# A delta-rule recurrence with a gated MLP: the first phase written out as one plan for all engines

## The chip, the cores and the metric

The kernel runs on one core of one Trainium2 chip. The metric is device time in microseconds for one execution. The engines are PE (TensorE, matmuls and its weight loads), DVE (VectorE), ACT (ScalarE), POOL (GpSimd) and SP (SyncE, which here issues transfers). Each works through its own list of instructions in order and waits on semaphores for the others. The order of each list is settled when the program is built.

## The reference

The first part is a recurrence over 768 tokens for 4 batches of 8 heads, with a 40 x 40 state per head:

```python
for t in range(S):
    y[:, :, t] = np.einsum('bhd,bhde->bhe', rt, state)
    Sa = np.einsum('bhde,bhe->bhd', state, at)
    state_decay = state * wt[:, :, None, :] - np.einsum('bhd,bhe->bhde', Sa, bt)
    state = state_decay + np.einsum('bhd,bhe->bhde', vt, kt)
```

The second part takes y, with the heads side by side, as x (4 x 768 x 320):

```python
h = np.maximum(x @ w_in, 0.0)
u, v = (h[..., :d_ff // 2], h[..., d_ff // 2:])
v_n = (v - mu) / np.sqrt(var + 1e-06)
v_s = np.einsum('ts,bsd->btd', w_spatial, v_n) + b_spatial[None, :, None]
return ((u * v_s) @ w_out)
```

## The kernel before

**Phase 1** (from L211) works on chunks of 64 tokens. Two batches go together: a step s handles 16 heads, as two groups g of four units n, where a unit has one head in the lower 64 partitions (par 0) and one in the upper (par 1). There are 24 steps: 12 chunks for each pair of batches. Inside a chunk the recurrence is a triangular system, so each step falls into parts.

- *Preparation* of chunk q (prep_steps, L309): a load into `ein`, two running products over the decays on VectorE (S, L318, and Et, L328), a small transfer of the chunk's total decay to DRAM (scr, L326), and the scaled operands `at` (L335) and `sl` (L338). lprime (L348) multiplies them into 32 x 32 triangular blocks, and lblock (L363, eviction at L368) masks these into Lc.
- *Inverse* (invert, L373): for four chunks at once, VectorE transposes the blocks, does thirty pairs of a multiply (L381) and an add (L385), and transposes the result twice (X11 at L389, XT0 at L392).
- *Bulk* products that don't need the state: b_lka (L420) with its mask on VectorE (L439), b_h (L444), b_tok (L458), and b_l21, b_zt, b_x21 with b_xcopy, which put together the 64 x 64 inverse `xf` from 32-wide parts. `xf` is stored 128 wide, with the two heads of a unit as diagonal blocks.
- *Chain* (chain, L517): four stages for each group, handing on from one to the next. bp multiplies the state (L540) and ScalarE copies it to Rt (L546); ff (L551) is copied to ffs (L556), and POOL masks the h part of Rt (L559); xx (L566) multiplies by the inverse and goes back into Rt, up to step 5 as a ScalarE copy (L573) with a POOL mask (L574), later as a ScalarE copy of the last 40 columns (L580) and a VectorE multiply by a mask (L581); mp (L590) updates the state Mc on VectorE (L595, L596), which ScalarE copies into Ms (L598), 128 wide with two diagonal blocks; y is finished at L601 and scaled at L609.

The *MoE* input layer (the reference's x @ w_in) runs beside phase 1, from stored y, in units: m_u (L714, 48 units) and m_v (L671, 24 units, followed by the normalization). Its weights come as 64-bit words and are decoded by VectorE (decode64, L69). In both units the last of eight products reads 64 partitions. **Phase 2** (L105) multiplies by w_spatial (pg, L172 to L174) and w_out (po, L192).

The order of the work is the tile framework's planner's: the code emits the chain's stages and lists of tasks by numbered slots (eight a step, from the constants at the top), and the planner orders each engine's list by its own cost model, with phase 2 included. The one exception is the start, where VectorE keeps the written order. All preparations from chunk 4 on use one load buffer, `ein[0]`; the other three serve only the first four chunks. All transfers are issued by SP's queue.

## Time and profile before

| | |
|---|---|
| median of 3 runs | 806.27 us (805.7 to 807.37) |
| span of the profiled execution | 803.9 us |
| instructions | 24058 |
| PE busy | 661.0 us (82%), 10016 matmuls |
| DVE busy | 489.7 us (61%), 992 |
| ACT busy | 413.1 us (51%), 960 |
| POOL busy | 289.4 us (36%), 449 |
| moved by DMA | 78.23 MB, mean 97 GB/s |

The profiled execution's own time beside its span is not in the page; the median of the runs lies 2.4 us above the span. A row of the groups has the line, the engine, the operation, out<-in, the shapes and the count, then the busy time in us and the mean of one in ns, then the idle time of the engine before these instructions and what ended it. Matmul records overlap (each runs through the array while the next starts), so their durations add up to more than they take. One fp32 matmul shows as two records. In a row in order of time the first two numbers are its start and its length in us.

### The profile page before, as it was taken

What the parts mean: (1) busy time and instruction counts of PE and PEld (TensorE: products, weight loads), DVE (VectorE), ACT (ScalarE), POOL (GpSimd) and SP (SyncE); (2) the same over time, 40 slices, a digit from 0 to 9 for tenths busy, and PEclk for the clock granted to TensorE, in tenths of its full rate; (3) what the DMA queues carried; (4) which work ended last, traced back from release to release, by engine and by line L of the source; (5) the groups of instructions that cost most, each with busy time, mean ns of one, the idle gap of its engine ahead of it and who ended that gap; (6) DMA issues with size and microseconds to landing.
All of it is one profiled execution on the core that took longest, in us unless ns stands there. A gap on an engine that the chain in (4) does not pass through costs nothing.

```text
span 803.9 us, 24058 instructions
## 1 busy us (share of the span) xinstructions
PE 661.0 (82%) x10016; PEld 571.2 (71%) x10016; DVE 489.7 (61%) x992; ACT 413.1 (51%) x960; POOL 289.4 (36%) x449
## 2 busy tenths in 40 slices
PE   1620575865989687988899899999999999999997
PEld 1520464654777575876777778787878898999997
DVE  7849358897389563898459874987232753232221
ACT  6210454333767184665675577778877243232112
POOL 5320455443435132332142331212143587353221
PEclk9965678555999799898899999999999999999999
DMA  7631355442354545352554444333342655153001
GB/s 169 100 44 39 38 95 120 100 79 54 101 96 59 108 84 107 94 97 58 102 86 111 89 125 125 93 102 115 103 124 73 192 184 177 64 173 106 31 25 50
DMA packets 113944, 78.23 MB, mean 97 GB/s; under 512 B 46844, under 2 KB 103420, under 8 KB 111996
## 3 DMA queue, kind: packets, MB, share of 16 engines
q1 hardware_dynamic: 113836, 76.70, 40.9%
q8 instruction: 79, 1.29, 0.8%
q14 instruction: 29, 0.24, 0.2%
HBM read 56.16 MB, written 20.51 MB: 95 GB/s over the span
## 4 chain that ended last, share of the span: by engine, by line
PE 47%; DVE 19%; DMA 16%; ACT 6%; issue 5%; POOL 5%; SPq 1%; DVEq 0%; POOLq 0%; ACTq 0%
DMA ein<-in_early 10%; PE po L192 5%; PE pv L714 5%; PE bp L540 5%; PE pv L671 4%; DVE A L385 4%; DVE itmp L381 3%; PE pg L173 3%; PE pg L174 3%; PE pg L172 3%; PE ch L551 3%; PE bk L450 2%; PE bp L601 2%; DVE S L318 2%; PE ch L566 2%
## 5 line engine op out<-in xcount | busy, mean ns | idle before, releaser
L338 POOL TENSOR_TENSOR sl<-ein,S 128x512 f32<-128x512 f32 x44 | 56.6, 1305 | 99.3 <-DVE S L318 57.3
L385 DVE TENSOR_TENSOR A<-A,itmp 128x30 f32<-128x30 f32 (+9 forms) x180 | 77.2, 429 | 4.2
L381 DVE TENSOR_TENSOR itmp<-A 128x30 f32<-128x30 f32 (+9 forms) x180 | 73.2, 407 | 4.6
L551 PE MATMUL ch<-Rt,At 128*64 128x104 f32 x768 | 57.2, 270 | 12.7 <-issue 12.4
L318 DVE TENSOR_TENSOR_SCAN S<-ein,ends 128x528 f32<-128x528 f32 x24 | 30.8, 1282 | 58.3 <-DMA ein<-in_early 54.6
L176 DVE TENSOR_TENSOR g<-pg,bb 128x384 f32<-128x384 f32 x32 | 17.7, 555 | 77.9 <-PE pg L174 71.1
L172 PE MATMUL pg<-wsh,vh 128*128 128x384 f32 x192 | 65.1, 339 | 0.0
L173 PE MATMUL pg<-wsl,vh 128*128 128x384 f32 x192 | 64.8, 338 | 0.0
L174 PE MATMUL pg<-wsh,vl 128*128 128x384 f32 x192 | 64.7, 337 | 0.0
L566 PE MATMUL ch<-ffs,xf 128*128 128x104 f32 x384 | 58.9, 303 | 6.3 <-ACT ffs L556 6.1
L540 PE MATMUL bp<-lin,Ms 128*104 128x104 f32 x384 | 53.9, 295 | 8.9 <-DMA lin<-in_late 4.2
L335 POOL TENSOR_TENSOR at<-ein,Et 128x256 f32<-128x256 f32 x40 | 27.9, 718 | 87.7 <-DVE Et L328 30.4
L566 PEld LDWEIGHTS ch<-ffs,xf 128*128 128x128 f32 x384 | 52.4, 211 | 9.9 <-ACT ffs L556 7.5
L551 PEld LDWEIGHTS ch<-Rt,At 128*64 128x64 f32 x768 | 43.5, 143 | 19.7 <-issue 14.9
L546 ACT ACTIVATE Rt<-bp 64x416 f32<-64x416 f32 x96 | 48.9, 510 | 15.2 <-PE bp L540 13.3
L358 PE MATMUL bk<-at,sl 64*32 64x32 f32 x1536 | 28.3, 208 | 34.2 <-POOL sl L338 9.9
L540 PEld LDWEIGHTS bp<-lin,Ms 128*104 128x104 f32 x384 | 47.1, 201 | 12.8 <-issue 7.9
L66 POOL TENSOR_TENSOR gl<-g,gh 128x384 fp32r<-128x384 f32 x32 | 33.3, 1042 | 59.6 <-ACT gh L62 59.6
L559 POOL TENSOR_SCALAR_AFFINE_SELECT Rt<-Rt 64x256 f32<-64x256 f32 x96 | 42.0, 438 | 32.1 <-PE ch L551 26.7
L418 ACT ACTIVATE xf<-XT 32x256 f32<-32x256 f32 x96 | 39.7, 414 | 23.8 <-DVE XT L392 22.5
L358 PEld LDWEIGHTS bk<-at,sl 64*32 64x32 f32 x1536 | 21.2, 119 | 40.6 <-issue 25.6
L601 PE MATMUL bp<-Rt,tk 128*40 128x64 f32 x768 | 43.0, 236 | 7.5 <-DVE Rt L581 5.0
(130 smaller groups left out, 1677.4 us busy)
## 6 DMA issues: line engine op xcount, KB each, us to landing
ein<-in_early SPq DMA_DIRECT2D x46, 322.5 KB
lin<-in_late SPq DMA_DIRECT2D x48, 160.0 KB
uts<-ur SPq DMA_DIRECT2D x48, 128.0 KB
vns<-vr SPq DMA_DIRECT2D x24, 256.0 KB
raw<-vns SPq DMA_DIRECT2D x24, 256.0 KB
ut<-uts SPq DMA_DIRECT2D x24, 256.0 KB
Rt<-in_vtok SPq DMA_DIRECT2D x48, 80.0 KB
xs<-y SPq DMA_DIRECT2D x48, 80.0 KB
```

The lines of the kernel that those rows point to most:

```text
L172: nc.tensor.matmul(pg, lhsT=vh[:, dc], rhs=w_h, start=(i == 0), stop=False)
L173: nc.tensor.matmul(pg, lhsT=vh[:, dc], rhs=w_l, start=False, stop=False)
L174: nc.tensor.matmul(pg, lhsT=vl[:, dc], rhs=w_h, start=False, stop=(i == NT - 1))
L338: st["sl"] = sl_eng[g].tensor_tensor(out=sl[:, gp], in0=oth[:, gp, 1:], in1=sv[:, gp, 2:C + 2].unsqueeze(2).broadcast_to([P, NP, 2, C]), o ...
L358: nc.tensor.matmul(pl[o:o + HB, n, :], lhsT=sl[PR[par], n, par, cs], rhs=at[PR[par], n, cs], start=True, stop=True,)
L381: nc.vector.tensor_tensor(out=tp, in0=A[:, k + 1:, k:k + 1].broadcast_to([P, m, k]), in1=A[:, k:k + 1, 0:k].broadcast_to([P, m, k]), op=AL ...
L385: nc.vector.tensor_tensor(out=A[:, k + 1:, 0:k], in0=A[:, k + 1:, 0:k], in1=tp, op=ALU.add)
L540: nc.tensor.matmul(bp[LV, q, :], lhsT=Ms[:, n, LV], rhs=li[:, n, C:], start=(q == 0), stop=False, skip_group_check=True,)
L546: nc.scalar.activation(Rt[par][rows, gp, :], bp[rows], AF.Copy)
L551: nc.tensor.matmul(ff[PR[1 - par], q, :], lhsT=At[par][:, n, :], rhs=Rt[par][:, n, :], start=True, stop=True,)
L566: nc.tensor.matmul(xx[:, q, :], lhsT=xf[:, n, :], rhs=ffs[:, q, :], start=True, stop=True,)
L601: nc.tensor.matmul(bp[RR[par], q, 0:C], lhsT=tk[:, n, par, :], rhs=Rt[par][:, n, 0:C], start=False, stop=True, skip_group_check=True,)
```

## The change

Phase 1 is rewritten as one list of (time, function) entries, `plan`, with times in steps: at(3.55, c_xx, 3, 0) is stage xx of step 3. The list is sorted, and up to step 24 it is emitted inside a region in which **every** engine keeps the written order (`manual_schedule()` without a list of engines). What comes later, the rest of the MoE and phase 2, is still the planner's.

- Each stage of the chain is cut into its products (c_bp, c_ff, c_xx, c_mp, c_y) and their evictions (c_..._out), and the two groups run side by side: both groups' bp, then both groups' ff, with bulk products and MoE units between.
- The state Mc is kept 64 wide and read directly: bp is two 40-row, 64-column products a unit instead of one of 128 rows and 104 columns, and Ms and its ScalarE copies are gone. The inverse xf is 64 wide too: xx is two 64 x 64 products a unit instead of one 128 x 128. xf's first copies move from ScalarE to POOL (on ScalarE for chunk 0), three instead of four.
- The mask after xx is POOL's in every step (TRI_ACT = 99), after a ScalarE copy of all columns. The mask on h moves from the chain to b_h_out, over both groups at once.
- Preparations use two load buffers in turn, `ein[0]` and `ein[1]`, loads have 48 rows instead of 40 (64 in the first four), and from chunk 4 on POOL does at and sl in one instruction each. The first loads go over SP's and ScalarE's queues, with scan inputs first; the fills of buffers and the zeroing of Ms, Rt, lin go away. scr is stored straight from S.
- Each inverse is spread evenly over the plan: the first whole, right after the first four preparations, the second from 2.5 to 3.45, the later ones over some three steps each. XT0 is now written before X11.
- Weight decoding is cut into single instructions (steps 3.3 to 10.2). The MoE starts at step 11 with four units a step. Before it started at step 5 with six units every two steps. The last product of a unit reads 128 partitions.

The core of the diff (the bodies of ff, mp and y are those of chain, cut apart; bulk functions are split the same way):

```diff
-CHB, MMB = 3, 1
-MOE_LAG = 32
-DEC0, DEC_STEP, DEC_OPEN = 5, 1, 2
-PREP_LAG, LP0, LP1, LPB = 10, 1, 3, 6
-PREP_SLOTS, PREP_AFTER = (0, 0, 6, 7), (False, False, True, True)
-PREP_OFF = (3, 4, 5)
-INV_SLOTS = (15, 17)
-LKA_ACT, TRI_ACT = 1, 6
-FIRST_SLOTS = ((0, 2, 2), (4, 5, 5, 6, 11, 12, 13), (10, 11, 11, 12, 14, 14, 15))
-BULK_OFF = (0, 0, 0, 1, 3, 1, 4, 4, 3, 1)
-MOE_OFF = (2, 1, 2, 3, 3, 3, 8, 3)
+LKA_ACT, TRI_ACT = 2, 99
...
-def decode64(nc, pool, h, l, src, n, bufs=1):
-    raw = pool.tile([P, n], I64, name="d_raw", bufs=bufs)
+def decode64_steps(nc, pool, h, l, src, n, bufs=1):
+    raw = pool.tile([P, n], I64, name="d_raw", bufs=2)
     nc.sync.dma_start(out=raw, in_=src)
+    yield
...
-    late_pool = late_bufs.enter_context(tc.tile_pool(name="late", bufs=1))
-    ein = [p.tile([P, EW], F32, name=f"ein{i}") for i, p in enumerate((pin, late_pool, extra, extra))]
+    ein = [p.tile([P, EW], F32, name=f"ein{i}") for i, p in enumerate((pin, pin, extra, extra))]
...
-    Ms = const.tile([P, NU, P], F32, name="Ms")
-    Mc = const.tile([P, NU, E], F32, name="Mc")
-    xfs = [const.tile([P, NU, P], F32, name=f"xf{i}") for i in range(2)]
+    Mc = const.tile([P, NU, C], F32, name="Mc")
+    xfs = [const.tile([P, NU, C], F32, name=f"xf{i}") for i in range(2)]
...
-    def prep_load(s, i=0, rows=E, cols=slice(0, EW)):
+    def prep_load(s, rows, cols=slice(0, EW), i=None, queues=(nc.sync, nc.sync)):
+        t = ein[s % 2 if i is None else i]
         for par in range(2):
             o = par * 64
-            nc.sync.dma_start(out=ein[i][o:o + rows, cols], in_=early[par, s, 0:rows, cols])
+            queues[par].dma_start(out=t[o:o + rows, cols], in_=early[par, s, 0:rows, cols])
...
+    def strict(t, k):
+        nc.gpsimd.affine_select(
+            out=t, in_=t, pattern=[[0, k], [1, C]], base=0, channel_multiplier=-1,
+            compare_op=ALU.is_gt, fill=0.0,
+        )
...
+    def b_h_out(s, par):
+        ev = PR[1 - par]
+        Rt = Rts[s % 2]
+        nc.scalar.activation(Rt[par][ev, :, 0:C], st["ph", s][ev], AF.Copy)
+        strict(Rt[par][ev, :, 0:C], NU)
...
+    def b_xcopy(s, eng):
+        XT0, X11 = st["X", s // GS]
+        us = slice((s % GS) * NU, (s % GS) * NU + NU)
+        xf = xfs[s % 2]
+        eng(out=xf[:, :, HB:], in_=XT0[:, us])
+        for o in (0, 64):
+            eng(out=xf[o:o + HB, :, 0:HB], in_=XT0[o:o + HB, us])
...
+    def c_bp(s, g):
+        gp, ns = grp(g)
         li = lin[s % 2]
+        bp = ps_b.tile([P, NP, NR], F32, name=f"bp{g}")
+        for q, n in enumerate(ns):
+            for par in range(2):
+                nc.tensor.matmul(
+                    bp[PR[par], q, :], lhsT=Mc[RR[par], n, :], rhs=li[RR[par], n, C:],
+                    start=(q == 0), stop=False, skip_group_check=True,
+                )
+        st["bp", g] = bp
+    def c_bp_out(s, g):
+        gp, ns = grp(g)
+        Rt = st["blk", s][1]
+        for par in range(2):
+            nc.scalar.activation(Rt[par][PR[par], gp, :], st["bp", g][PR[par]], AF.Copy)
...
+    def c_xx(s, g):
+        gp, ns = grp(g)
+        xf = st["blk", s][3]
+        ffs = st["ffs", g]
+        xx = ps_c.tile([P, NP, NR], F32, name="ch")
+        for q, n in enumerate(ns):
+            for ev in PR:
+                nc.tensor.matmul(
+                    xx[ev, q, :], lhsT=xf[ev, n, :], rhs=ffs[ev, q, :], start=True, stop=True,
+                )
+        st["xx", g] = xx
+    def c_xx_out(s, g):
+        gp, ns = grp(g)
+        Rt = st["blk", s][1]
+        xx = st["xx", g]
+        for par in range(2):
+            ur, ev = PR[par], PR[1 - par]
+            if s < TRI_ACT:
+                nc.scalar.activation(Rt[par][ur, gp], xx[ev], AF.Copy, scale=-1.0)
+                strict(Rt[par][ur, gp, 0:C], NP)
+                continue
+            nc.scalar.activation(Rt[par][ur, gp, C:], xx[ev, :, C:], AF.Copy, scale=-1.0)
+            nc.vector.tensor_tensor(
+                out=Rt[par][ur, gp, 0:C], in0=xx[ev, :, 0:C],
+                in1=maskn[ev].unsqueeze(1).broadcast_to([64, NP, C]), op=ALU.mult,
+            )
...
+    def c_mp_out(s, g):
+        gp, ns = grp(g)
+        if s % CPB == CPB - 1:
+            if s < NS - 1:
+                nc.vector.memset(Mc[:, gp, 0:E], 0.0)
+            return
+        mp = st["xx", g][:, :, C:]
+        mn = jit.tile([P, NP, E], F32, name="mn")
+        nc.vector.tensor_tensor(out=mn[LV], in0=mp[LV], in1=Mc[LV, gp, 0:E], op=ALU.add)
+        nc.vector.tensor_tensor(
+            out=Mc[LV, gp, 0:E], in0=mn[LV], in1=st["scn"][LV, gp, :], op=ALU.mult
+        )
...
-        mm += [(xh[:, k, g, :], wl[:, k, vc]) for k in range(2)]
-        mm += [(xh[0:64, 2, g, :], wl[0:64, 2, vc])]
+        mm += [(xh[:, k, g, :], wl[:, k, vc]) for k in range(3)]
...
+    M1, M2, M3, M4 = 0.22, 0.46, 0.65, 0.80
+    for s in range(NS):
+        at(s + 0.02, scn_load, s)
+        for g in range(NB):
+            at(s + 0.00 + 0.05 * g, c_bp, s, g)
+            at(s + 0.04 + 0.05 * g, c_bp_out, s, g)
+            at(s + 0.30 + 0.05 * g, c_ff, s, g)
+            at(s + 0.34 + 0.05 * g, c_ff_out, s, g)
+            at(s + 0.55 + 0.05 * g, c_xx, s, g)
+            at(s + 0.60 + 0.05 * g, c_xx_out, s, g)
+            at(s + 0.74 + 0.02 * g, c_mp, s, g)
+            at(s + 0.755 + 0.02 * g, c_mp_out, s, g)
+            at(s + 0.86 + 0.04 * g, c_y, s, g)
+            at(s + 0.90 + 0.04 * g, c_y_out, s, g)
+            at(s + 0.95 + 0.01 * g, y_store, s, g)
+    for q in range(1, NS):
+        b = q - 1
+        for par in range(2):
+            at(b + 0.11 + 0.02 * par, b_copy, q, par)
+            at(b + 0.17 + 0.02 * par, b_lka_out, q, par)
+            at(b + 0.72 + 0.02 * par, b_h_out, q, par)
+            at(b + 0.40 + 0.03 * par, b_tok, q, par)
+            at(b + 0.43 + 0.03 * par, b_tok_out, q, par)
+        at(b + 0.115, b_lka, q)
+        at(b + 0.52, b_l21, q)
+        at(b + 0.54, b_l21_out, q)
+        at(b + 0.66, b_zt, q)
+        at(b + 0.68, b_zt_out, q)
+        at(b + 0.68, b_h, q)
+        at(b + 0.50, b_xcopy, q, p.tensor_copy)
+        at(b + 0.78, b_x21, q)
+        at(b + 0.81, b_x21_out, q)
+    for q in range(2, NS):
+        at(q - 2 + 0.14, lin_load, q)
+        at(q - 2 + 0.97, vtok_load, q)
+    LPO = 0.93
+    PREP = {4: 0.03, 5: 0.45, 6: 1.03, 7: 1.45, 8: 2.03, 9: 2.45, 10: 3.03, 11: 3.45}
+    for q in range(GS, NS):
+        t = PREP.get(q, q - 8 + 0.01)
+        at(t + 0.20, scan1, q)
+        at(t + 0.28, scan2, q)
+        at(t + 0.285, scr_store, q)
+        at(t + 0.29, at_mul, q, p)
+        at(t + 0.30, sl_mul, q, p)
+        if q + 2 < NS:
+            at(t + 0.50, prep_load, q + 2, 48)
+        at(t + LPO, lprime, q)
+        at(t + LPO + 0.05, lblock, q)
+    for g in range(1, NS // GS):
+        t0 = 2.5 if g == 1 else max(4.5, GS * g - 4 + 0.0)
+        t1 = GS * g - 1 + 0.45
         gen = invert(g)
+        for k in range(INV_N):
+            at(t0 + (t1 - t0) * k / (INV_N - 1), step, gen)
+    T_DEC, T_MOE = 4.2, 11
     for i in range(6):
+        gen = decode(1 - i // 3, i % 3)
+        for k in range(9):
+            at(T_DEC + i + k * 0.12 - (0.9 if k == 0 else 0), step, gen)
+    at(T_DEC + 5.9, open_act)
+    slots = [T_MOE + k // 4 + (M1, M2, M3, M4)[k % 4] for k in range(3 * NS)]
+    for j in range(NS // 2):
+        bq, i = j // 6, j % 6
+        own = slots[6 * j:6 * j + 6]
+        at(max(own[0] - 1.6, 2 * j + 2.1, T_DEC + 5.92), m_load, bq, i)
+        at(max(own[0] - 0.7, 2 * j + 2.7), m_split, bq, i)
+        for t, d in zip((own[0], own[1], own[3], own[4]), range(DH // P)):
+            at(t, m_u, d, bq, i)
+        for t, g in zip((own[2], own[5]), range(NB)):
+            at(t, m_v, g, bq, i)
+            at(t + 0.14, m_n1, g)
+            at(t + 0.42, m_root, g)
+            at(t + 0.48, m_n2, g)
+            at(t + 0.76, m_n3, g, bq, i)
...
-    with tc.manual_schedule(engines={mybir.EngineType.DVE}):
+    with tc.manual_schedule():
+        W, O = slice(0, WF), slice(WF, EW)
+        qs = (nc.sync, nc.scalar)
+        for cols, q in ((W, 0), (W, 1), (O, 0), (W, 2), (O, 1), (W, 3), (O, 2), (O, 3)):
+            prep_load(q, 64, cols, q, qs)
+        lin_load(0)
...
+        for q in range(GS):
+            scan1(q, q)
+            scan2(q)
+            if q:
+                scr_store(q)
+            at_mul(q, p)
+            sl_mul(q, p, g0)
+            sl_mul(q, v, g1)
+            lprime(q)
+            if q:
+                lblock(q - 1)
+            if q == 0:
+                b_copy(0, 0)
...
+        lblock(GS - 1)
+        lin_load(1)
+        vtok_load(1)
+        prep_load(4, 48)
+        prep_load(5, 48)
         for _ in invert(0):
             pass
...
+        plan.sort()
+        n = 0
+        while plan[n][0] < NS:
+            t, _, fn, args = plan[n]
+            fn(*args)
+            n += 1
+    for t, _, fn, args in plan[n:]:
+        fn(*args)
```

627 lines of the change are left out of this document (244 added, 383 removed).

## The prediction

> **What bounds the kernel now.** I read the page from the top, then the chain of waits, then stretches of the span, and last the groups of instructions.
>
> ```profile
> span 803.9 us, 24058 instructions
> PE   1620575865989687988899899999999999999997
> PEclk9965678555999799898899999999999999999999
> ```
>
> Each digit is a twentieth of 40 us. From the 23rd slice on (about 440 us) TensorE is busy nine tenths or more at full clock; before that it has holes, and for the first 200 us the granted clock is often 0.5 to 0.7. So there are two problems: an early part that waits, and a late part that is bound by TensorE.
>
> ```profile
> PE 47%; DVE 19%; DMA 16%; ACT 6%; issue 5%; POOL 5%; SPq 1%; DVEq 0%; POOLq 0%; ACTq 0%
> ...
> 51.06 1.26 DVE L318 TENSOR_TENSOR_SCAN S<-ein,ends 128x528 f32<-128x528 f32 x1 [12.60 <-DMA ein<-in_early]
> 76.44 1.86 DVE L392 STREAM_TRANSPOSE XT<-A 128x1024 f32<-128x1024 f32 x1
> 95.37 1.26 DVE L318 TENSOR_TENSOR_SCAN S<-ein,ends 128x528 f32<-128x528 f32 x1 [12.06 <-DMA ein<-in_early]
> 102.36 0.42 DVE L609 TENSOR_TENSOR y<-bp,Et 104x256 f32<-104x256 f32 x1 [1.22 <-PE bp L601]
> 205.56 0.39 DVE L609 TENSOR_TENSOR y<-bp,Et 104x256 f32<-104x256 f32 x1
> 484.63 0.42 DVE L609 TENSOR_TENSOR y<-bp,Et 104x256 f32<-104x256 f32 x1
> 616.75 0.42 DVE L609 TENSOR_TENSOR y<-bp,Et 104x256 f32<-104x256 f32 x1
> ```
>
> Transfers are a sixth of the chain. The lines below the dots are VectorE in order of time. It stops twice for 12 us, in the middle of the first inverse and again in step 0, for a scan whose load is not there. One buffer feeds every later preparation, so a load starts only when the products of the chunk before have been read. L609 ends a step's second group: step 0 at 102.8 us, step 3 at 205.9, step 15 at 485.0, step 22 at 617.2. The last seven of these steps took 132.1/7 = 18.9 us each. The stretches say what filled them (core time, then busy us of PE, PEld, DVE, ACT, POOL, each with its count, clock, DMA share, GB/s):
>
> ```profile
> 126.00:206.00 80.00, 51.39 (x843) 42.26 (x834) 68.08 (x127) 28.67 (x64) 34.63 (x39) 0.64 0.40 85
> 485.00:617.00 132.00, 130.12 (x2263) 107.67 (x2263) 74.30 (x181) 103.90 (x244) 31.22 (x68) 1.00 0.37 106
> 643.00:804.00 161.00, 156.43 (x928) 149.48 (x926) 47.85 (x83) 44.92 (x96) 67.89 (x80) 1.00 0.32 101
> ```
>
> Steps 2 and 3 are VectorE's: 68 of 80 us. Steps 16 to 22 are TensorE's: 130 of 132. So is what follows the last step.
>
> **Start and step 0.** The first inverse now follows the four first preparations with no later scan inside it. Before it ended at 76.44 + 1.86 = 78.3 us. I take away the wait of 12.6 and the scan pair in it (1.28 + 1.67 + 0.2 for the reciprocal, 3.2): 62 us. The four chunks are loaded with 64 rows instead of mostly 40, but on two queues and without VectorE's and POOL's fills; the inverse's start at about 31 us leaves that room. From the inverse to the end of step 0 it was 24.5 us, 12.1 of it the second wait: 12 left, a little less since the XT transpose is now first. **Step 0 ends at 73**, 30 earlier. Two buffers, each refilled nearly two steps ahead, hide the later loads; they cost at most the old wait if the load is late in steps 0 to 3.
>
> **VectorE's steps.** The rows (busy us, mean ns of one):
>
> ```profile
> L385 DVE TENSOR_TENSOR A<-A,itmp 128x30 f32<-128x30 f32 (+9 forms) x180 | 77.2, 429 | 4.2
> L381 DVE TENSOR_TENSOR itmp<-A 128x30 f32<-128x30 f32 (+9 forms) x180 | 73.2, 407 | 4.6
> L328 DVE TENSOR_TENSOR_SCAN Et<-ein,ends 128x528 f32<-128x528 f32 x24 | 40.0, 1667 | 0.3
> L439 DVE TENSOR_TENSOR At<-bk,maskp 64x512 f32<-64x512 f32 x46 | 31.7, 689 | 24.3 <-PE bk L426 23.5
> L318 DVE TENSOR_TENSOR_SCAN S<-ein,ends 128x528 f32<-128x528 f32 x24 | 30.8, 1282 | 58.3 <-DMA ein<-in_early 54.6 <-POOL wl L102 3.4 <-ACT wc L324 0.3
> L581 DVE TENSOR_TENSOR Rt<-ch,maskn 64x256 f32<-64x256 f32 x72 | 30.4, 422 | 27.6 <-ACT Rt L580 25.9
> L609 DVE TENSOR_TENSOR y<-bp,Et 104x256 f32<-104x256 f32 x48 | 19.8, 414 | 6.0 <-PE bp L601 5.7 <-remote 0.2
> L679 DVE BATCH_NORM_STATS2 bs<-vr 128x6 f32<-128x512 f32 x24 | 16.4, 683 | 13.4 <-ACT vr L673 13.2
> L596 DVE TENSOR_TENSOR Mc<-mn,scn 104x160 f32<-104x160 f32 x44 | 15.7, 357 | 0.3
> L700 DVE TENSOR_SCALAR vr<-vr,mv,q 128x512 f32<-128x512 f32 x24 | 14.8, 622 | 11.5 <-POOL q L695 11.0
> L595 DVE TENSOR_TENSOR mn<-ch,Mc 104x160 f32<-104x160 f32 x44 | 13.9, 317 | 11.5 <-PE ch L590 9.4 <-remote 1.8
> L389 DVE STREAM_TRANSPOSE X<-A 128x1024 f32<-128x1024 f32 x6 | 12.0, 1993 | 0.2
> L368 DVE TENSOR_TENSOR Lc<-bk,maskl 128x256 f32<-128x256 f32 x24 | 9.9, 411 | 11.1 <-PE bk L358 7.3 <-PE bp L540 3.7
> ...
> 100.00:200.00 100.00, 25.85 (x42) 0.65 0.44 89
> ```
>
> The last line is VectorE on the weight decoding alone: 25.85/6 = 4.3 us a block. A step's fixed work is 1.28 + 1.67 + 0.2 (one preparation) + 2 x 0.689 + 0.41 + 2 x (0.317 + 0.357) + 2 x 0.414 = 7.1, 7.6 with half a microsecond between instructions. An inverse is 30 x (0.429 + 0.407) + 3 x 2.0 = 31, 33 with its gaps. L581 goes away: its mask is POOL's now.
>
> - Step 1: two preparations, 11; TensorE has 13.4 (below): **14**.
> - Steps 2 and 3: two preparations each and the whole second inverse, 2 x 11.2 + 33 = 55; **57** with waits.
> - Steps 4 to 7: 30.4 + 33 + four decoded blocks at 4.5 = 82; **86**.
> - Steps 8 to 11: 30.4 + 33 + two blocks = 72; **76**.
> - Steps 12 to 15: 30.4 + 33 + four units of the MoE a step (0.683 + 0.622 and two small ones, 1.7 for three units, so 2.3 a step) = 73; TensorE needs the same there: **78**.
>
> The microsecond a step that I add in steps 2 to 11 is for hand-overs: VectorE's evictions of lka and of mp stand in a fixed order and wait if TensorE is late. While they wait, the scans and the inverse behind them wait too, and POOL's products behind those.
>
> **TensorE's steps.** The group of L', then rows in order of time, inside steps 16 and 17 and after the last step:
>
> ```profile
> L358 PE MATMUL bk<-at,sl 64*32 64x32 f32 x1536 | 28.3, 208 | 34.2 <-POOL sl L338 9.9
> ...
> 508.99 0.93 PE L551 MATMUL ch<-Rt,At 128*64 128x104 f32 x16
> 511.76 1.14 PE L566 MATMUL ch<-ffs,xf 128*128 128x104 f32 x8
> 522.42 0.98 PE L540 MATMUL bp<-lin,Ms 128*104 128x104 f32 x8
> ...
> 711.68 0.52 PE L714 MATMUL pv<-xh,wh 128*128 128x256 f32 x3
> 712.04 0.40 PE L714 MATMUL pv<-xl,wh 128*128 128x256 f32 x2
> 712.27 0.71 PE L714 MATMUL pv<-xh,wl 128*128 128x256 f32 x3
> 712.91 0.45 PE L173 MATMUL pg<-wsl,vh 128*128 128x384 f32 x1
> 713.19 0.34 PE L174 MATMUL pg<-wsh,vl 128*128 128x384 f32 x1
> ```
>
> The state and inverse products become sixteen pieces 64 wide. The nearest form is L551, sixteen in 0.93: xx gains 0.21 a group (0.4 a step), bp 0.05 (0.1). Bounds: half of 0.93 if two quadrants run at once, 1.14 if they gain nothing. The MoE's last product reads 128 rows instead of 64. The first five of the unit at 711.68 started in 0.59 us, 0.118 each, so eight should take 0.94; the next line's work started 1.23 later and then stumbled by 0.11 more (0.28 between starts where 0.17 is usual). That is 0.4 a unit, 1.2 for the three units of a step. A fourth unit a step adds a third of (2 x 0.94 + 1.8) = 1.2. The hand order also runs each product whole, where the planner cut several into parts with another form between; I count 13 fewer changes of form a step. Between nothing and 0.2 each (half of the 0.4); I take 1.1 a step, nearer to the lower end, as most changes are not to 64 rows of 128 columns. Sum: 18.9 - 0.4 - 0.1 - 1.2 + 1.2 - 1.1 = 17.3. L' (absent from step 16 on) adds at most 28.3/24 = 1.2, its records overlapping; I take 0.9. Without the MoE: 17.3 - 4.8 + 0.9 = 13.4.
>
> ScalarE had 103.9/7 = 14.8 a step here. It loses the Ms and xf copies and gains wider Rt copies and one unit's eviction: it stays under 15 of 17.3, but is the next to be late. POOL's rows, one mask and the preparation's product (shortest, median, longest):
>
> ```profile
> L574 POOL TENSOR_SCALAR_AFFINE_SELECT Rt<-Rt 64x256 f32<-64x256 f32 x24 | 11.4, 476 | 6.4 <-ACT Rt L573 5.5
> ...
> L338 POOL TENSOR_TENSOR sl<-ein,S x44: 1170/1184/2133, 8.4 to 469.7; 128x512 f32<-128x512 f32 x44
> ```
>
> POOL had 31.2/7 = 4.5 a step in the late stretch. It gets four masks at 0.48 and three xf copies that the trace does not show: nearest the mask, 0.4 each, at most 1.2 like the product. About 8 of 17.3, hidden by TensorE unless it holds a mask that mp waits for; with that cover gone, the 3.1 a step would show, 25 us over steps 16 to 23. The two masks of h replace four half as wide. **Steps 16 to 23: 8 x 17.3 = 138.**
>
> **The end.** The MoE starts at step 11 with four units a step: 52 of 72 done when step 23 ends, 20 left, 160 matmuls, and phase 2's 864. Before, 928 took 161 us, with 15 broken units (6 us) and 3 for the last store: 0.164 each. 1024 x 0.164 + 3 = **171**, 10 more than before.
>
> **Sum.** 73 + 14 + 57 + 86 + 76 + 78 + 138 + 171 = 693 us of span. The median stands 806.27 - 803.9 = 2.4 above the profiled span: **695 us**.
>
> **Rivals.**
>
> *The clock.* In steps 2 to 11 TensorE has 13.4 of some 22 us to do, with one hole of several microseconds before bp, while VectorE finishes. At 126 to 206 us the same picture had a clock of 0.64. Then 13.4 becomes 20.9, and VectorE waits for lka and mp, some 3 us a step for ten steps: 725. For it: that row. Against: slices of 0.8 and 0.9 later, with TensorE at eight tenths. The Trainium skill (TensorE: Matmul & The Clock Gate, Part 1: The HAM clock gate) says that one idle window of about 3.4 us sends the array to half clock; the trace agrees in kind with the 0.64 here.
>
> *VectorE and POOL in each other's way.*
>
> ```profile
> L328 DVE TENSOR_TENSOR_SCAN Et<-ein,ends x24: 1215/1258/2315, 6.5 to 463.0; 128x528 f32<-128x528 f32 x24
> ```
>
> The same scan takes 1.2 or 2.3 us, the same product on POOL 1.2 or 2.1: they sometimes exclude each other. My means contain that at today's load. POOL will have 8.6 a step in steps 2 to 15 (the two sl products 2.4, the two of at 1.4, the masks 3.6, the copies 1.2). If all of it fell on VectorE, and a third of it is in the means, these steps take 5.7 more: 14 x 5.7 = 80, 775. Against: most scans are at the short end. The Trainium skill (SBUF — State Buffer, Who interferes with whom) has it as a rule, that a VectorE instruction with two SBUF inputs shuts out one of GpSimd that reads SBUF; by it the masks moved from VectorE, which read PSUM, cost VectorE part of what they save.
>
> *Only the start gains.* If the planner already packed what comes after step 3 as well as can be, steps 0 to 3 end at 144 instead of 206 and the end is 10 longer: 806 - 62 + 10 = 754. For it: nines from 440 us. Against: between 206 and 440 the slices aren't full.
>
> *Slower: the hand order exposes every eviction.* TensorE's order is fixed, so a stage that finds its eviction undone stops all behind it. One group is bp 0.93, two copies, ff 0.93, a copy, xx 0.93, two copies and a mask, mp and its two VectorE instructions: about 8 us; both one after the other 16, bulk products 6, units 5: 27 a step. With 24 in steps 1 to 11: 73 + 264 + 12 x 27 + 171 = 832. It is slower than now once steps 1 to 23 average over (804 - 73 - 171)/23 = 24.3; I forecast 19.5. Against: three to five microseconds of other products stand between a stage and its successor.
>
> **Chances.** Forecast 0.54 (its own range 665 to 720: the form changes alone give -18 to +13, 64-wide pieces at half price another -13); clock 0.14; only the start 0.13; VectorE against POOL 0.10; exposed evictions 0.08; 0.01 that it ends level. Range 655 to 775. About 0.2% (1.6 us) is what a measurement can tell from no change. Faster 0.91, same 0.01, slower 0.08.
>
> **What would show it.** Right: no DMA wait ahead of scans after the start; the first inverse done near 62; steps 4 to 11 with VectorE over nine tenths busy, 16 to 23 with TensorE; y of step 23 at 522. Wrong: clock under 0.7 in steps 4 to 11; inverse instructions longer than 0.43 on average; TensorE below nine tenths in steps 16 to 23 with waits on ScalarE's copies or POOL's masks, which would put the fault in the hand order.

## The result and the profile after

The changed kernel takes 782.83 us (median of 4 runs, 778.59 to 784.71); the kernel before, timed beside it, takes 806.82. The ratio is 0.969, 95% interval 0.965 to 0.973: faster, but by 24 us and not by the 111 forecast, and 8 us above the range. Its profiled execution has a span of 776.9 us. From the page of the changed kernel:

```profile
span 776.9 us, 25305 instructions
PE   0434676567676976779899789999999999589997
PEclk9985967658877696789689779999999999989999
DMA  9360787737567664564545544435426352353001
```

TensorE is full from the 25th slice on, but for the 35th and 36th; before, it was full from the 24th on. The early slices are better but not full. The granted clock is mostly lower than before from the 11th to the 24th slice. The same execution cut where the forecast cut it (core time, busy us of PE, PEld, DVE, ACT, POOL with counts, clock, DMA share, GB/s):

```profile
0.00:82.00 82.00, 30.29 (x785) 26.49 (x786) 51.87 (x99) 22.30 (x47) 28.80 (x45) 0.85 0.51 97
82.00:108.00 26.00, 17.18 (x476) 15.34 (x463) 9.59 (x17) 10.68 (x22) 11.28 (x15) 0.80 0.87 92
108.00:172.00 64.00, 38.40 (x978) 34.64 (x966) 54.81 (x98) 21.25 (x44) 26.29 (x28) 0.68 0.64 89
172.00:260.00 88.00, 63.19 (x1591) 56.56 (x1588) 78.57 (x140) 43.31 (x91) 42.12 (x50) 0.77 0.67 108
260.00:354.00 94.00, 72.90 (x1611) 64.88 (x1612) 74.39 (x128) 47.24 (x97) 45.63 (x54) 0.76 0.52 88
354.00:453.00 99.00, 84.08 (x1714) 74.09 (x1712) 73.96 (x145) 52.60 (x114) 46.86 (x76) 0.82 0.52 114
453.00:599.00 146.00, 142.55 (x2728) 124.67 (x2727) 80.82 (x185) 106.27 (x227) 71.80 (x147) 0.99 0.46 133
599.00:777.00 178.00, 162.49 (x964) 157.47 (x962) 55.59 (x99) 47.91 (x103) 72.43 (x94) 0.98 0.31 99
```

These are step 0, step 1, steps 2 and 3, 4 to 7, 8 to 11, 12 to 15, 16 to 23, and the end. In steps 1, 8 to 11 and 12 to 15 no engine is full, so no engine's own work fills them, and waits decide. TensorE's longest wait between 82 and 600 us, and all of its waits that end with "issue" (engine, line, waited for: us in total, times, longest):

```profile
PE bp L528 <- DVE y L630: 22.2, 8, 8.8
PE bk L325 <- issue: 10.5, 6, 2.6
PE ch L593 <- issue: 7.1, 7, 2.0
PE bk L388 <- issue: 6.5, 3, 3.4
PE bk L434 <- issue: 5.8, 1, 5.8
PE bp L617 <- issue: 4.5, 2, 2.3
PE bk L470 <- issue: 2.8, 2, 1.9
PE bk L418 <- issue: 2.7, 3, 1.7
PE bp L528 <- issue: 2.0, 1, 2.0
PE bk L451 <- issue: 0.8, 1, 0.8
```

"issue" is a wait that nothing in the profile explains. The rows with it add up to 42.7 us. I call them **stops**. The kernel before has 14.3 us of them in the same steps (102 to 643 us there):

```profile
PE bk L358 <- issue: 7.3, 3, 4.8
PE bp L540 <- issue: 2.6, 2, 1.4
PE bk L510 <- issue: 2.1, 3, 0.9
PE bk L450 <- issue: 2.0, 1, 2.0
PE ch L551 <- issue: 0.3, 1, 0.3
```

One stop of the changed kernel, in TensorE's order of time, step 11:

```profile
329.50 0.63 PE L388 MATMUL bk<-at,sl 64*64 64x64 f32 x16
333.58 0.69 PE L388 MATMUL bk<-at,sl 64*64 64x64 f32 x8 [3.44 <-issue]
```

It stops for 3.44 us within a group of 16 independent products (32 records). VectorE's eviction of this group waits 5.5 us (the longest of five between 192 and 354 us, below), and the step takes 26.4 us where its neighbours take 21.4 and 21.6.

```profile
DVE At L408 <- PE bk L388: 8.4, 5, 5.5
```

Start and step 15 have waits of their own. VectorE at chunk 3, then POOL behind it, then ScalarE in step 15:

```profile
29.91 1.26 DVE L282 TENSOR_TENSOR_SCAN S<-ein,ends 128x528 f32<-128x528 f32 x1 [8.84 <-DMA scr<-S]
41.27 0.42 DVE L336 TENSOR_TENSOR Lc<-bk,maskl 128x256 f32<-128x256 f32 x1 [7.65 <-PE bk L325]
41.73 1.94 DVE L344 STREAM_TRANSPOSE A<-Lc 128x1024 f32<-128x1024 f32 x1
```

```profile
36.42 1.37 POOL L395 TENSOR_SCALAR_AFFINE_SELECT Rt<-Rt 64x512 f32<-64x512 f32 x2 [10.04 <-ACT Rt L427]
```

```profile
444.79 0.84 ACT L52 ACTIVATE wsh<-raw 128x768 fp32r<-128x768 f32 x1 [7.24 <-DMA raw<-in_wspT]
```

S has two buffers, and scr is stored straight from it, so chunk 3's scan waits until the store of chunk 1 has read the buffer. Then POOL's products of chunk 3 stand behind the masks of h in the fixed order. The first inverse starts at 41.7 us, not 31.

Of two kernels below (the splits held behind step 16, and the first run with 40-row loads) the profiled execution was a disturbed one; their ratios are of undisturbed runs.

### The profile page after: what moved, and what is told of

Same layout as the page of the kernel before. It is cut to its first block, busy times and chain, and to the rows that moved or that the text cites. A ratio compares the mean times of both kernels' runs of the same rounds, so it can differ in the third digit from the quotient of the medians.

```text
span 776.9 us, 25305 instructions
## 1 busy us (share of the span) xinstructions
PE 611.1 (79%) x10784; PEld 554.1 (71%) x10784; DVE 479.6 (62%) x905; ACT 351.6 (45%) x745; POOL 345.2 (44%) x505
## 4 chain that ended last, share of the span: by engine, by line
PE 42%; DVE 3%; ACT 3%; issue 3%; DMA 2%; POOL 1%; SPq 1%; ACTq 0%; DVEq 0%
PE po L195 6%; PE pv L684 5%; PE pv L729 5%; PE pg L175 4%; PE pg L176 4%; PE pg L177 4%; PE bp L528 3%; PE ch L546 2%; PE ch L564 2%; PE bk L434 1%; PE bp L617 1%; PE bk L388 1%; PE bk L418 1%; DMA uts<-ur 1%; PE bk L497 1%
## 5 line engine op out<-in xcount | busy, mean ns | idle before, releaser
L395 POOL TENSOR_SCALAR_AFFINE_SELECT Rt<-Rt 64x512 f32<-64x512 f32 (+1 forms) x144 | 79.7, 557 | 52.6 <-ACT Rt L427 26.3
L306 POOL TENSOR_TENSOR at<-ein,Et 128x512 f32<-128x512 f32 x24 | 30.4, 1265 | 112.4 <-DVE Et L291 69.1
L528 PE MATMUL bp<-lin,Mc 40*64 40x104 f32 x768 | 54.7, 308 | 24.7 <-DVE y L630 22.2
L528 PEld LDWEIGHTS bp<-lin,Mc 40*64 40x64 f32 x768 | 48.2, 172 | 27.8 <-DVE y L630 24.5
L176 PE MATMUL pg<-wsl,vh 128*128 128x384 f32 x192 | 64.9, 338 | 0.0
L576 ACT ACTIVATE Rt<-ch 64x416 f32<-64x416 f32 x96 | 49.1, 511 | 13.7 <-PE ch L564 6.5
L325 PE MATMUL bk<-at,sl 64*32 64x32 f32 x1536 | 24.4, 219 | 38.5 <-POOL sl L312 24.4
L312 POOL TENSOR_TENSOR sl<-ein,S 128x1024 f32<-128x1024 f32 (+1 forms) x24 | 52.2, 2175 | 0.0
L325 PEld LDWEIGHTS bk<-at,sl 64*32 64x32 f32 x1536 | 20.6, 130 | 42.7 <-POOL sl L312 25.2
L408 DVE TENSOR_TENSOR At<-bk,maskp 64x512 f32<-64x512 f32 x44 | 30.3, 689 | 30.1 <-PE bk L388 29.3
L546 PE MATMUL ch<-Rt,At 128*64 128x104 f32 x768 | 47.4, 283 | 0.0
L564 PE MATMUL ch<-ffs,xf 64*64 64x104 f32 x768 | 45.0, 274 | 0.0
L470 PE MATMUL bk<-XT,l 32*32 32x32 f32 x768 | 19.0, 199 | 32.9 <-DVE XT L359 28.7
```

What stands on the lines that cost most here:

```text
L176: nc.tensor.matmul(pg, lhsT=vh[:, dc], rhs=w_l, start=False, stop=False)
L312: eng.tensor_tensor(out=sl[:, ns], in0=oth[:, ns, 1:], in1=sv[:, ns, 2:C + 2].unsqueeze(2).broadcast_to([P, k, 2, C]), op=ALU.mult,)
L395: nc.gpsimd.affine_select(out=t, in_=t, pattern=[[0, k], [1, C]], base=0, channel_multiplier=-1, compare_op=ALU.is_gt, fill=0.0,)
L528: nc.tensor.matmul(bp[PR[par], q, :], lhsT=Mc[RR[par], n, :], rhs=li[RR[par], n, C:], start=(q == 0), stop=False, skip_group_check=True,)
L546: nc.tensor.matmul(ff[PR[1 - par], q, :], lhsT=At[par][:, n, :], rhs=Rt[par][:, n, :], start=True, stop=True,)
L564: nc.tensor.matmul(xx[ev, q, :], lhsT=xf[ev, n, :], rhs=ffs[ev, q, :], start=True, stop=True,)
```

## The experiments

Ratios are to the kernel before, timed on the same chip, with their 95% interval. Its medians there lie between 806.7 and 813.2 us, and the changed kernel was not timed beside them again, so I read differences under a per cent from the steps. "Stops" is the sum of TensorE's issue waits between 82 and 600 us. Edits are to the changed kernel unless another is named.

**Hand order or planner.**

```diff
-    with tc.manual_schedule():
+    with tc.manual_schedule(engines={mybir.EngineType.DVE}):
```

> Only VectorE keeps its hand order through the first phase; the queues of the other engines are left to the planner, as in the kernel before. The changed kernel took 0.969 of the kernel before (span 776.9 us). Theory A, the hand order on all engines is what shortens the steps, and its flaws (a mask or a load queued ahead of what is needed) cost less than it brings: the ratio goes back to 0.98 or more, with steps 2 to 15 longer than the changed kernel's 344 us in sum. Rival B, the order of POOL, ScalarE and SyncE is what was lost against the forecast: the ratio falls below 0.96, and steps 4 to 15 (281 us in sum) lose 15 us or more.

Measured 0.981 (0.970 to 0.992), stops 24.4 us, steps 2 to 15 348 us in sum. By the number this is theory A, but the interval meets the changed kernel's and the steps are 4 us longer in sum: the fixed order of the four other engines is worth little.

**The clock.** `heat` issues six matmuls of ident by ident into the unread tile pv.

```diff
+    for s in range(0, 11):
+        for f in (0.855, 0.995):
+            at(s + f, heat, s)
```

> Twelve more fp32 matmuls of ident by ident a step, six ahead of bp and six ahead of y, in steps 0 to 10, into a PSUM tile that nobody reads. They take 12 x 0.28 us = 3.4 us of TensorE a step if nothing is idle there, by the 281 ns of the 128x128 transposes. Theory A, the clock bounds steps 4 to 11: the granted clock between 192 and 354 us goes from 0.75 to over 0.9, the mean of a bp matmul (L528 of the changed kernel) from 334 ns to under 280 ns, and steps 4 to 11 lose 10 us or more of their 182 us. Rival B, VectorE bounds these steps (its busy time is 127 us of the 135 between 192 and 327 us): the clock rises just so, but steps 4 to 11 stay within 4 us of 182. Rival C, TensorE itself is the bound: the steps grow by up to 3.4 us each, 30 us in sum, and the ratio to the kernel before goes over 1.0.

Measured 0.977 (0.966 to 0.987). Steps 4 to 7 in this kernel:

```profile
181.00:269.00 88.00, 71.48 (x1730) 65.11 (x1722) 79.55 (x140) 43.50 (x91) 41.53 (x50) 0.86 0.67 108
```

The clock went from 0.77 to 0.86, bp's mean to 253 ns, and the four steps take 88.8 us for 88.0, with the same 79 us of VectorE. Steps 8 to 11 take 94.5 for 93.8. Rival B: the clock doesn't bound these steps. The Trainium skill (TensorE: Matmul & The Clock Gate, Part 1: The HAM clock gate) has the clock follow how busy TensorE was; this run agrees, and shows that a better clock need not be time.

**The second phase's weights in step 15.** The first run holds their loads, splits and decodes behind step 17 (`tc.issue_after` on four engines); the second holds ScalarE's and VectorE's parts alone, behind step 16.

```diff
+    for ins in hold:
+        held.enter_context(tc.issue_after(ins))
```

> The second phase's weight loads, splits and decodes are queued behind the masks, evictions and stores of step 17 on SyncE, ScalarE, VectorE and POOL; the changed kernel has the first of them in step 15. Theory A: step 15 goes from 29.8 us to 18 to 22, its clock stays above 0.9, nothing is given back, and the whole loses 8 to 11 us (ratio 0.955 to 0.959). Rival B: the same waits come up in steps 18 to 21, which are now 17 us, or at the start of the second phase, and the whole stays within 3 us of the changed kernel (0.965 to 0.972). Rival C: step 15 is long from its clock alone and stays at 28 or more.

> ScalarE's and VectorE's parts of the second phase's weights are queued behind an eviction and a product of step 16; the loads stay where they were, so that they land ahead of the splits. Held behind step 17 with their loads, step 15 fell from 29.8 to 18.9 us and step 18 rose from 17.3 to 27.1. Theory A, it is the wait for the load at the head of ScalarE's and VectorE's queues, and a later split finds its data: step 15 at 18 to 21, no step from 16 to 22 above 21, the whole 7 to 10 us shorter than the changed kernel. Rival B, the loads themselves start later in this order and the wait moves again: one of the steps 16 to 19 above 24 and the whole within 3 us.

Measured 0.974 (0.966 to 0.982), step 15 at 18.9 us but step 18 at 27.1: rival B, the 10 us come up again. The second measured 0.951 (0.941 to 0.962); its steps 15 to 17 took 23.9, 22.4 and 19.9, 66.2 us for 66.0. Its runs lie between 768 and 788 us, the profiled one at the upper end, so here ratio and steps do not agree and it stays open whether that hold gains.

**POOL's order.**

```diff
-        at(t + 0.29, at_mul, q, p)
-        at(t + 0.30, sl_mul, q, p)
+        at(t + 0.675, at_mul, q, p)
+        at(t + 0.676, sl_mul, q, p)
```

> POOL's two products of a chunk's preparation (at and sl, 1.27 and 2.18 us) are queued behind the masks of xx, not ahead of them, in steps 0 to 15. Theory A, the masks stand on the path of y there: the wait of y's matmuls on POOL (6.0 us of L617 between 192 and 354 us) goes, and steps 4 to 15 lose 8 us or more of 281; the loads of the next chunks start some 7 us later in a step without a new wait. Rival B, VectorE or the clock bounds these steps whatever POOL does: within 4 us of 281, and another wait (VectorE's on the second L' products, or TensorE's on sl) takes the place of the 6.0 us.

Measured 1.013 (1.004 to 1.022). The load of chunk q + 2 into the same buffer, at t + 0.50, now stands ahead of the products, so they read chunk q + 2's inputs (the results are then not the chunks' own) and wait for them, 91.3 us in sum. This tells nothing on the masks, only that products that wait for their load cost some 35 us in the whole.

**POOL beside VectorE.**

```diff
-        at(t + 0.29, at_mul, q, p)
-        at(t + 0.30, sl_mul, q, p)
+        at(t + 0.29, at_mul, q, v)
+        at(t + 0.30, sl_mul, q, v)
```

> The two products of each chunk's preparation, at and sl, go from POOL (1.24 and 2.26 us) to VectorE in steps 0 to 15 (0.68 us for 128x512 there, so 2.0 us a step). In the changed kernel the 60 products of an inverse take 20.7 us with POOL quiet (chunks 0 to 3) and 32.2 and 35.2 with POOL busy 0.41 and 0.53 of the time (second and third group after it); fitted over all inverses, a microsecond of a two-operand product on POOL beside them adds 0.7 to 0.9 us, a mask 0.45, a copy 0.3. Theory A, POOL's two-operand products stop VectorE, and VectorE bounds steps 4 to 10: these two inverses fall to 29 us or less, VectorE loses nothing in sum, POOL's masks come earlier, and steps 4 to 15 (281 us) lose 8 us or more. Rival B, the longer inverses come from something else: they keep their 32 and 35 us, VectorE has 2.0 us more a step and steps 4 to 10 (155 us) gain up to 14 us in length.

Measured 0.960 (0.952 to 0.968). The inverse's instructions, in the changed kernel and then in this one:

```profile
L354 DVE TENSOR_TENSOR A<-A,itmp 128x30 f32<-128x30 f32 (+9 forms) x180 | 84.7, 470 | 6.1
L350 DVE TENSOR_TENSOR itmp<-A 128x30 f32<-128x30 f32 (+9 forms) x180 | 79.4, 441 | 3.0
```

```profile
L354 DVE TENSOR_TENSOR A<-A,itmp 128x30 f32<-128x30 f32 (+9 forms) x180 | 71.7, 398 | 6.2
L350 DVE TENSOR_TENSOR itmp<-A 128x30 f32<-128x30 f32 (+9 forms) x180 | 69.8, 388 | 3.0
```

The third and fourth inverse fell from 32.2 and 35.2 us to 25.7 and 28.8. VectorE gave the same back as at and sl, and steps 4 to 15 took 286 us for 281, with 55.8 us of stops. The contention is real; under these transfers its removal buys nothing in those steps. The Trainium skill (SBUF — State Buffer, Who interferes with whom) says that a VectorE instruction with two SBUF inputs contends with a GpSimd one that reads SBUF, over ports that only one of them holds at a time. The trace agrees for POOL's products (0.7 to 0.9 us lost per us beside them, by a fit), but only by half for its masks (0.45).

**The start.** A ScalarE copy `wc` of the column is stored in place of S, and b_h(0) with its masks moves behind chunk 3's products.

```diff
-            nc.sync.dma_start(out=scr[s, par].rearrange("n e -> e n"), in_=sv[RR[par], :, 1])
+            nc.sync.dma_start(out=scr[s, par].rearrange("n e -> e n"), in_=wc[RR[par]])
```

> Two repairs ahead of step 0: ScalarE copies the column of S that is stored to scr, so that the store no longer holds S (the changed kernel's scan of chunk 3 waited 8.84 us for it), and b_h(0) with its two masks on POOL comes behind the products of chunk 3. Theory A, these two made the start late: the first inverse begins near 33 us instead of 41.7, step 0 ends near 74 instead of 82.3, the later steps keep their lengths, and the whole loses 6 to 9 us (0.96 of the kernel before). Rival B, step 1 waits for its own loads and takes the gain back: step 1 still ends within 3 us of 108.3 and the whole stays. Rival C, the small copies on ScalarE in steps 1 to 15 cost as much as they save in S: step 0 gains, steps 1 to 15 lose.

Measured 0.958 (0.952 to 0.964). The first products of the inverse start at 33.9 us for 43.7, as expected. But step 0 ends at 81.3 for 82.3, since TensorE stops inside step 0's y:

```profile
73.74 0.53 PE L619 MATMUL bp<-Rt,tk 128*40 128x64 f32 x10
79.37 1.44 PE L619 MATMUL bp<-Rt,tk 128*40 128x64 f32 x22 [5.11 <-issue]
```

None of the three had this. The gain of the start is lost in step 0 itself, and the span (780.7 us) shows none.

**The transfers.** Four runs changed what is moved. First, no loads for chunks 8 to 23 (their results are then not the chunks' own):

```diff
-        if q + 2 < NS:
+        if q + 2 < 8:
```

> The loads of the inputs of chunks 8 to 23 (387 KB each) are left out, so their scans and products work on the inputs of chunks 6 and 7: the time is that of the kernel without this traffic. Idle time of TensorE in the middle of a group of independent matmuls, ended by nothing that the profile shows, is 42.7 us between 82 and 600 us, 14.3 in the kernel before; a transfer of 16 KB of instructions lies at several of these places. Theory A, the loads hold up TensorE's instructions and so lengthen steps 11 and 13: that idle time falls under 20 us, steps 11 and 13 (26.4 and 28.3 us) go to 22 or less, and steps 4 to 15 (281 us) lose 12 us or more. Rival B, VectorE and POOL block each other and TensorE's stops lie beside that: the idle time may fall, but steps 4 to 15 stay within 5 us of 281.

Measured 0.943 (0.936 to 0.950), stops 28.2 us. Step 11 went from 26.4 to 20.1, step 13 only to 26.0, steps 4 to 15 to 271 us. Theory A in part. Then 40 rows in place of 48, run twice, and additional traffic:

```diff
-            at(t + 0.50, prep_load, q + 2, 48)
+            at(t + 0.50, prep_load, q + 2, E)
```

> Each load of a chunk's inputs brings 40 rows a half, as in the kernel before, in place of the changed kernel's 48 (8 of them padding that is in the buffer already): 645 KB a chunk for 774. In the changed kernel one chunk's load takes 7 to 8 us, and in the kernel before 4.7 to 5.3, more than the bytes explain. Without any such load (chunks 8 to 23) steps 4 to 15 took 271 us for 281 and TensorE's idle time ended by nothing shown 27.8 us for 42. Theory A, the load's time on the queues holds up TensorE's instructions: that idle time falls to 36 us or less, steps 4 to 15 lose 4 us or more, the whole 4 to 10 us. Rival B, the eight rows are free and only the number of loads counts: steps 4 to 15 within 3 us of 281.

> The 40-row loads alone once more, for a profile: the profiled run of the first one was disturbed. Theory A (the small elements): TensorE's idle time ended by nothing shown stays above 30 us, and what the loads gain is found in waits for their data. Theory B (the 48-row loads): it falls to 15 us or less, and the mean of an 8256-byte packet from 899 ns to about the 555 ns of the kernel before. Theory C: between.

```diff
+            nc.sync.dma_start(out=dump[s % 2][par], in_=early[par, s, 0:48])
```

> Each of the steps 1 to 15 also copies a chunk's inputs (2 x 387 KB) from DRAM to DRAM, where nobody reads them; no engine's work changes. Theory A, the transfers' share of the queues holds up TensorE's instructions: the idle time of TensorE ended by nothing shown rises from 42 us to 55 or more between 82 and 600 us, and steps 1 to 15 (370 us) grow by 15 us or more. Rival B, the loads matter only where an engine waits for their data: that idle time stays within 6 us of 42, and what steps 1 to 15 grow by is found in waits for a DMA.

The 40 rows measured 0.951 (0.946 to 0.957) and 0.953 (0.944 to 0.962), stops 34.2 us. The additional 12 MB measured 0.970 (0.967 to 0.974), stops 51.2 us, and steps 1 to 15 at 372 us for 370: more stops than rival B allowed, but none of the time of theory A. So the 12 MB of copies in large pieces are nearly free. The eight rows of padding in each load are not: without them steps 4 to 15 took 268 us for 281. But 34.2 us of stops are left: theory A of the first run, and by the stops theory A of the second. That left the small pieces: each chunk's store to scr is 640 elements of 4 bytes.

```diff
-    scr = dscr.tile([NS, 2, NU, E], F32, name="scr")
+    scr = dscr.tile([NS, 2, E, NU], F32, name="scr")
...
-            nc.sync.dma_start(out=scr[s, par].rearrange("n e -> e n"), in_=sv[RR[par], :, 1])
+            nc.sync.dma_start(out=scr[s, par], in_=wc[RR[par]])
```

> One part of the cheaper transfers alone on the changed kernel: the column of S is copied by ScalarE and stored in scr as 80 rows of 32 bytes a chunk in place of 640 elements of 4 bytes; the loads keep 48 rows and b_h(0) its place. The three parts together took TensorE's idle time ended by nothing shown from 42 to 3.0 us and the whole to 0.914 of the kernel before; the copy with b_h(0)'s place left that idle time at 46 us. Theory A, the small elements hold up TensorE's instructions: the idle time falls to 20 us or less, and the whole to 0.945 or less. Theory B, the 48-row loads do (the 40-row loads alone came to 0.951): the idle time stays above 35 us, and the whole at 0.955 or more. Theory C, each does its part: 20 to 35 us, 0.94 to 0.955.

Measured 0.926 (0.920 to 0.933). All of TensorE's stops between 82 and 600 us in this kernel:

```profile
PE bk L327 <- issue: 7.1, 3, 3.7
PE bp L530 <- issue: 2.8, 1, 2.8
PE ch L595 <- issue: 1.0, 2, 0.7
PE bk L390 <- issue: 0.2, 1, 0.2
```

42.7 us became 11.1, step 1 went from 26.0 to 17.2, step 11 to 17.4, and the whole lost 34 us: theory A. The edit also frees S by ScalarE's copy; that copy, with b_h(0) moved, had left the stops at 47.2 (**The start**), and the run of the kernel before, below, changes the layout alone. All three repairs together, and the same with at and sl on VectorE:

> Fewer and cheaper transfers: the 40-row loads, the repaired start (the column of S copied by ScalarE, b_h(0) behind chunk 3's products), and that column stored in scr as rows of 32 bytes, 80 for a chunk, in place of 640 of 4 bytes; VectorE then reads scn with a stride of eight. Theory A, transfers bound the start and steps 1 to 3 through TensorE's instructions: steps 0 to 3 end at 160 us or less for 171.9, steps 4 to 15 at 273 or less, and the whole comes to 0.945 of the kernel before or less. Rival B, each of the three is hidden: the whole stays at 0.96 or more. The strided read costs VectorE at most the time of the product again, 0.7 us a step.

> The cheaper transfers with at and sl on VectorE besides, so that POOL no longer stands in VectorE's way with them. With the changed kernel's transfers that move shortened the inverses by 6.5 us each and cost 2.0 us a step on VectorE, with nothing gained. Theory A, VectorE's own work bounds steps 4 to 10 and POOL's share of it is now its own: within 4 us of the run with the cheaper transfers alone. Rival B, POOL's at and sl stood on the path of TensorE's second L' products: 5 us or more better than that run.

Measured 0.914 (0.910 to 0.918) with 3.0 us of stops, and 0.899 (0.896 to 0.902) with 9.5. The first met theory A. The second is 13 us better again, rival B by its number; most of it lies in step 0 (4.5), step 3 (2.1) and steps 12 to 15 (7.1). Whether L' is what waited there I did not separate. Last, the store by rows in the kernel before:

> The kernel before with one edit: its column of S, copied by ScalarE there already, is stored in scr as 80 rows of 32 bytes a chunk in place of 640 elements of 4 bytes, and read with a stride of eight. TensorE's idle time ended by nothing shown is 14 us in the kernel before and 42 in the changed one, of which the same edit takes 31 away. Theory A, small elements hold up TensorE in any order of the work, only less where the order leaves more idle time: the kernel before loses 8 us or more (0.99 or less), its idle time of this kind falls to 5 us or less. Theory B, it is the meeting of the small elements with the changed kernel's earlier and larger loads that hurts: the kernel before stays within 0.5%.

Measured 0.955 (0.950 to 0.961): the kernel before loses the same 4.5%. Its stops fall to 1.7 us, and VectorE's wait for loads, 54.6 us before, to this:

```profile
DVE S L318 <- DMA ein<-in_early: 26.5, 8, 8.7
```

Theory A. ScalarE made the copy there already, so the layout of the store is the only difference. The small elements were there before the change, and cost as much.

**What is left.** With the transfers repaired and at and sl on VectorE: the planner for the other engines; the MoE from step 9 (`T_DEC, T_MOE = 2.2, 9`); and that with the hold behind step 16.

> The kernel with the cheaper transfers and at and sl on VectorE (0.899), with VectorE alone in hand order and the other engines' queues left to the planner. Theory A, the hand order of TensorE, ScalarE, POOL and SyncE is worth some per cent once the transfers no longer stop TensorE: 0.915 or more. Rival B, the planner's queues do as well behind VectorE's order: 0.894 to 0.904.

> The kernel with the cheaper transfers and at and sl on VectorE (0.899), with the MoE's products from step 9 on instead of 11 and its weights' decode from 2.2 instead of 4.2. TensorE is busy 0.66 to 0.74 of steps 8 to 10 there and full from step 11 on. Theory A, those steps have room for eight units of some 2 us each: the tail loses 12 to 16 us, steps 2 to 8 change little as VectorE's sum is the same, and the whole comes to 0.88 to 0.885. Rival B, VectorE bounds steps 2 to 8 and the earlier decode lengthens steps 2 and 3 by what steps 8 to 10 gain, with MoE work on ScalarE and VectorE on top: the whole stays at 0.893 or more.

> The fastest kernel so far (0.886: cheaper transfers, at and sl on VectorE, the MoE from step 9), with ScalarE's and VectorE's parts of the second phase's weights queued behind step 16. In its step 15 (28.3 us) ScalarE waited 9.25 us for the first of these loads with the step's own evictions queued behind. Theory A, the wait goes, since the data is there by step 16: step 15 at 21 us or less and the whole at 0.876 to 0.88. Rival B, as in the changed kernel, where the same edit took 29.8 us to 23.9 and steps 16 and 17 gave it back (22.4 and 19.9 for 19.3 and 16.9), the gain is given back in steps 16 and 17: within 0.4% of 0.886.

Measured 0.902 (0.897 to 0.908), no different from 0.899; 0.886 (0.881 to 0.890), 714.48 us, the fastest and all but theory A's size; and 0.886 (0.879 to 0.894). The earlier MoE shortens the end from 178.6 to 156.5 us, and steps 2 to 15 give back 16 of that, 5 of it in step 3. In the last run step 15 fell from 28.3 to 16.8, and steps 16 and 17 took 21.4 each for 17.3 and 18.2: given back once more.

## Why the prediction was wrong

The blocks in us, by the ends of the steps' y; the last column has the cheaper transfers and at and sl on VectorE:

| block | forecast | changed | scr by rows | all three repairs | and at, sl |
|---|---|---|---|---|---|
| step 0 | 73 | 82.3 | 79.5 | 78.5 | 73.9 |
| step 1 | 14 | 26.0 | 17.2 | 17.9 | 17.6 |
| 2, 3 | 57 | 63.6 | 64.9 | 59.3 | 57.2 |
| 4 to 7 | 86 | 88.0 | 90.4 | 86.4 | 89.0 |
| 8 to 11 | 76 | 93.8 | 84.6 | 84.2 | 83.0 |
| 12 to 15 | 78 | 98.9 | 88.4 | 84.6 | 77.6 |
| 16 to 23 | 138 | 146.1 | 145.2 | 147.4 | 145.0 |
| end | 171 | 178.2 | 178.4 | 177.0 | 178.6 |
| span | 693 | 776.9 | 748.6 | 735.2 | 721.9 |

- **The step that failed** is "Two buffers, each refilled nearly two steps ahead, hide the later loads". VectorE's wait for loads did go (54.6 us to 8.0 us, 5.1 of it in step 1). But the forecast priced a transfer only by who waits for its data, and beside VectorE's and TensorE's own work it allowed a microsecond a step for hand-overs. Transfers also stop TensorE: this kernel has 42.7 us of such stops. Repairing the three transfers took 42 us off the span, 24 of it in steps 1 to 11 and 14 in steps 12 to 15. That is half of the 84 us by which the span missed. The kernel before paid for the small elements too: storing by rows took 28 us off VectorE's waits for loads there, and 13 off the stops.
- **Start and step 0** were missed by 9 us. The inverse ended at 70.1, not 62, for the scr store and the masks of h. With those repaired it ended 9 us earlier, and a stop took the gain. Step 0 came to 73.9 only with the transfers repaired and at and sl on VectorE.
- **VectorE's steps.** 4 to 7 came within 2 us, with VectorE busy 79 of 88. In 8 to 11 it is only 74 of 94. The inverse's instructions averaged 0.46 us, not 0.42, which is the sign named for a wrong forecast. That is the rival of VectorE and POOL: its mechanism is there, 49 us longer in all six inverses than their shortest instructions would take, 37 in the kernel before, so 12 more and not 80. The 775 lies near the result by luck: half of the miss is the transfers', and moving at and sl off POOL brought 13 us once these were repaired.
- **12 to 15** lacked step 15's wait for the second phase's load and the stops in step 13. With the transfers repaired and at and sl on VectorE they come to the 78 forecast.
- **TensorE's steps** held: 16 to 22 average 17.6 us for 17.3, and ScalarE and POOL are hidden. Step 23 takes 23.2, as such a step did before (25.5), and I had not set it apart. The end is 7 us over, and one wait is as long. At 682 us TensorE's next w_out products (po) need gh, which ScalarE makes behind a VectorE product, and that product waited for the load of ut:

```profile
681.65 0.99 ACT L52 ACTIVATE gh<-g 128x384 fp32r<-128x384 f32 x2 [4.33 <-DVE g L180]
682.23 0.63 PE L195 MATMUL po<-woh,gh 128*128 128x320 f32 x1 [7.01 <-ACT gh L52]
```

  The kernel before has 0.3 us of waits over 0.15 us in its end, and the kernels with the repaired transfers have the same 7 us. That this wait is the whole excess was not tested.
- **The clock** was low as that rival said (0.68 to 0.77 in steps 2 to 11), and raising it changed nothing in steps 4 to 11. **Only the start gains** named a time nearer to the result than the forecast's (754), but its shape is not there: steps 0 to 3 end at 171.9, not 144, and steps 2 to 15 became 14 us shorter. **Exposed evictions** did not show: steps 1 to 23 average 22.5 us, below the 24.3 named for it, and letting the planner order them gains nothing.
- With the transfers repaired and at and sl on VectorE 29 us stay over the forecast: 7 in steps 8 to 11, 7 in steps 16 to 23 (4 of it step 23), 8 in the end, 4 in step 1 and 3 in steps 4 to 7. Their causes, but for the wait in the end, stay open. Putting POOL's masks of xx back on VectorE was not tried.

## What to carry to other kernels

When no engine is full in a stage, add up the idle time that nothing explains, by engine, before looking at orders and buffers; a stop in the middle of a group of independent matmuls is the sign. Count a transfer's pieces as well as its bytes: 56 KB stored in 4-byte elements cost some 34 us here and 36 in the kernel before, 12 MB of extra copies in large pieces next to nothing. But look at padding too: eight rows in each load cost some 13 us. A wait that is pushed out of one step is gained only if the run shows the later steps unchanged.
